# An early copy of the next scores, and a gate that turns its tokens where the FFN summed them

## The chip, the cores and the metric

The kernel runs on one core of a Trainium2 chip. Its metric is the device time of one execution, in microseconds. In three runs the kernel before took 1214.4, 1216.44 and 1218.95 us, so its median is 1216.44 us. One more execution, the profiled one, took 1221.99 us; its program spans 1220.3 us.

## The reference, cut to what matters

Three stages follow one another on 2304 tokens of width 512: attention in which each query keeps its 32 largest scores (4 batches, 8 heads, 576 positions, head width 64), a feed-forward layer (FFN, 512 to 2048 to 512, with a slope for negative values), and a mixture of 8 experts with one expert per token, chosen by a gate.

```python
scores = q @ k.T / sqrt(D)                       # 576 x 576 for each of 32 heads
kth    = 32nd largest of each row
attn   = softmax(where(scores >= kth, scores, -1e9))
x      = (attn @ v) as 2304 x 512
h      = x @ w_in;  x2 = (max(h, 0) + alpha * min(h, 0)) @ w_out
logits = x2 @ w_gate + bias[modality]            # 2304 x 8
e      = argmax(logits);  out = p(e) * (relu(x2 @ w1[e]) @ w2[e])
```

## The kernel before, in words

**Steps.** The attention is cut into 72 steps of two tiles each; a tile is 128 queries of one head against 576 keys. The work of a tile is spread over several steps, so that each step holds a piece of work of five different pairs of tiles. The order of the instructions is written out by hand: the schedule is manual, each engine executes its own instructions in the order of the program, and semaphores hold an instruction back until what it reads is written and what it overwrites has been read. Nothing is reordered.

The FFN runs in the same loop. It works on chunks of 256 tokens (two row blocks r = 0, 1), eight of them, and two half chunks of 128 tokens. A full chunk takes eight steps, one pair of hidden blocks (`fp`) a step, so that a chunk ends in about every eighth step. After the loop the expert phase runs, about 25 us for each of nine blocks.

**One step s** of the main loop holds, in the order of the program (the letters in front are engines: PE for TensorE, ACT for ScalarE, DVE for VectorE, POOL for GpSimd):

- POOL `low` (L530, L531) for the two tiles of step s-2 and a transposing DMA; ACT `mask` (L518) and POOL `mask` (L519) for the two tiles of step s-1
- DVE `topk` of the pair s, about 30 instructions: three L466 that read the score banks `SC` and the copied scores `t.S` (the first writes its result into `SC`, columns 576 to 719), two L463, then maxima and replacements (L469, L493)
- DVE `slope` (L657), ACT and POOL `pair` (L664, L665) for the FFN's hidden block of the step before
- PE `mm2` (L678) for the hidden block of two steps before; where the chunk is complete, ACT `fin` (L685) copies the two sums `c.X2[r]` to `c.x2`
- PE `scores` (L445, L446) for the pair s+1, into the two halves of `SC`; PE `mm1` (L629) for the next hidden block, into the bank `psH`
- ACT `expo` (L522) for the two tiles of s-1; ACT `relus` (L643), which copies `psH`; ACT `keep_scores` (L449), which copies the scores of the pair s+1 from `SC` to `t.S`; ACT `high` (L526) for the two tiles of s-1
- the slot "mid", with what earlier steps put there (the gate, parts of the preparation of q, k and v); PE `av` (L550) for the pair s-3; the slot "late"

So DVE's first instruction on a pair waits for `keep_scores` of that pair, POOL's `low` of the next step waits for `high`, and the second exponential waits for the second mask of POOL.

**The FFN's sums.** `c.X2[r]` is one tile of 128 x 512 fp32 from the pool `psX`, which has two buffers. The next chunk's first `mm2` takes the same buffers, as soon as their last reader is through.

**The gate** turns each row block of `c.x2` by four PE transposes (`gate1`, L690), copies the result to SBUF (L692, ACT) and multiplies it by the gate's weights (`logits`, L696). Before, `gate1` writes the turned tokens to columns 720 to 975 of `SC`, 256 columns in each half. Row block 0 is turned in the slot "mid" of the step after the chunk's end, row block 1 one step later; `logits` follow one step after each. The copies go to the ring `gr` of four buffers, which `relus` uses too. For the last two chunks `gate1` is called for both row blocks together, in `after` and in `finish`.

Of the kernel before, what the change touches and what calls it, by code (L numbers as in the profile page):

```python
# [14 lines left out]
AF = mybir.ActivationFunctionType  # L15
# [45 lines left out]
def tile_kernel(ctx, tc, q, k, v, w_in, w_out, alpha, mod_id, w_gate, mod_bias, w1, w2, out, dbg=None, force=False):  # L61
    nc = tc.nc
    V, A, G, T, SY = nc.vector, nc.scalar, nc.gpsimd, nc.tensor, nc.sync
# [5 lines left out]
    bankO = psO.tile([128, 512], F32, name="bankO")  # L69

    SC = psO.tile([128, 2, 1024], F32, name="psS")
    X2AT, GATEAT = 576, 720
    SUMS, LOGITS, RANKS, COUNTS = 264, 272, 288, 304
    psH = ctx.enter_context(tc.tile_pool(name="psH", bufs=1, space=PSUM))
    psX = ctx.enter_context(tc.tile_pool(name="psX", bufs=2, space=PSUM))
# [7 lines left out]
    ident = const.tile([128, 128], F32, name="ident")  # L83
# [91 lines left out]
    def phase1(exact, ph, rc, rs, flags, ohs, mp):  # L175
# [15 lines left out]
        def at(slot, s_, f):  # L191
            hooks[slot].setdefault(s_, []).append(f)

        def hooked(slot, s_):
            while hooks[slot].get(s_):
                hooks[slot][s_].pop(0)()
# [25 lines left out]
        def flush():  # L222
            while fill:
                fill.pop(0)()
# [223 lines left out]
        def keep_scores(t):  # L448
            A.activation(t.S, SC[:, t.z, :S], AF.Copy, scale=LOWER)  # L449
# [71 lines left out]
        def expo(t):  # L521
            A.activation(t.S, t.S, AF.Exp, scale=t.c.negc, bias=t.b)  # L522
# [65 lines left out]
        def chunk(ci, xn, rs):  # L588
            ffn = state.ffn
            c = Rec()  # L590
# [94 lines left out]
                    A.activation(c.x2[:, r, :], c.X2[r], AF.Copy, scale=c.un[:, r:r + 1])  # L685

            def gate1(r):
                p_ = SC[:, :, GATEAT:GATEAT + 256]
                for cc in range(NCC):
                    T.transpose(p_[:, cc // 2, cc % 2 * 128:cc % 2 * 128 + 128], c.x2[:, r, cc * 128:cc * 128 + 128], ident)  # L690
                c.x2T[r] = ffn.tile([128, NCC, 128], F32, name="gr", bufs=GR)
                A.activation(c.x2T[r].rearrange("p (a c) t -> p a (c t)", a=2), p_, AF.Copy)  # L692

            def logits(r):
                for cc in range(NCC):
                    T.matmul(bankO[:, LOGITS + 8 * r:LOGITS + 8 * r + 8], c.x2T[r][:, cc, :], wg[:, cc, :],  # L696
                             start=(cc == 0), stop=(cc == NCC - 1))
# [64 lines left out]
            def place(r):  # L762
                G.memset(spacer, 0.0)
                d_ = G.indirect_dma_start(out=mapD, out_offset=bass.IndirectOffsetOnAxis(ap=c.si[:, r:r + 1], axis=0),
                                          in_=c.tg[:, r, :], in_offset=None)
                if r:
                    tc.declare_no_dep(d_.ins, c.placed.ins, reason="other slots")
                c.placed = d_
# [14 lines left out]
            def after(s_):  # L783
                if c.k == NCH:
                    return
                if c.k == NCH - 1:
                    for r in range(2):
                        gate1(r)
                        at("next", s_ + 1, lambda r=r: logits(r))
                    at("next", s_ + 1, gate2)  # L790
                    at("next", s_ + 1, gate2b)
                    at("mid", s_ + 1, gate3)
                    at("mid", s_ + 1, gate3b)
                    at("mid", s_ + 1, weight)
                    at("mid", s_ + 1, inverse)
                    at("late", s_ + 1, flush)
                    for r in range(2):
                        at("late", s_ + 1, lambda r=r: place(r))
                    at("mid", s_ + 2, lambda: first_block(s_ + 2))
                    return  # L800
                for r in range(R):
                    at("mid", s_ + 1 + r, lambda r=r: gate1(r))
                    at("mid", s_ + 2 + r, lambda r=r: logits(r))
                at("mid", s_ + GATE[0], gate2)
                at("mid", s_ + GATE[0] + 1, gate2b)
                at("mid", s_ + GATE[1], gate3)
                at("mid", s_ + GATE[1] + 1, gate3b)
                at("mid", s_ + GATE[2], weight)
                at("mid", s_ + GATE[2] + 1, inverse)
                for r in range(R):  # L810
                    at("late", s_ + GATE[2] + 2 + r, lambda r=r: place(r))
# [77 lines left out]
        def weights_for(fp):  # L889

            return wgroup.cn["high"] >= 2 * fp + 18
# [135 lines left out]
        s_ = -LOOK  # L1027
        while True:
            att_on = s_ < NIT + 4
            if s_ == NIT + 4:  # L1030
                atts.close()
            if not att_on and not (posted or paired or fpq or any(x >= s_ for h_ in hooks.values() for x in h_ if h_[x])):
                break
            state.alone = s_ >= NIT
            k1_, main = 0, []

            def run_main(n_):
                nonlocal k1_
                for _ in range(n_):
                    if k1_ < len(main):  # L1040
                        main[k1_]()
                        k1_ += 1

            prev = live.get(s_ - 1, [])
            if WL == 0 and s_ < 12:
                wgroup.load()
            hooked("early", s_)
            while factors:
                factors.pop(0)()
            for t in live.get(s_ - 2, []):  # L1050
                low(t)
            for t in prev:
                mask(t)
            while doubt:
                doubt.pop(0)()
            main = topk(live[s_]) if 0 <= s_ < NIT else []
            if WL == 1 and s_ < 12:
                wgroup.load()
            hooked("next", s_)

            run_main(MAIN0)
            if ended:
                kept_, fill[:] = fill[:], []
                while ended:
                    av_out(ended.pop(0))
                flush()
                fill[:] = kept_
            post = posted[:]
            del posted[:]
            for c, fp in post:  # L1070
                for f in c.slope(fp):
                    f()
            for c, fp in paired:
                if c.k == NCH and fp == c.n - 1:
                    mp.b0.mm(0, (0,))
                c.mm2(fp)
                if fp == c.n - 1:
                    c.fin()
                    at("mid", s_, lambda c=c, s_=s_: c.after(s_))
                    at("late", s_, c.keep)  # L1080
            del paired[:]
            for c, fp in post:
                c.pair(fp)
                paired.append((c, fp))
            nxt = []
            if s_ + LOOK < NIT:
                nxt = live[s_ + LOOK] = tile_pair(s_ + LOOK)
                for t in nxt:
                    scores(t)
            while fill and FILL0:  # L1090
                fill.pop(0)()
                run_main(1)
            n_ = 0
            credit = min(credit + (RATE[2] if s_ < NIT else 1), 1 if s_ >= NIT else 1 if exact else CRED) if fpq else 0
            while fpq and credit >= 1 and n_ < 2 and fpq[0][0] <= s_ and weights_for(fpq[0][2]):
                credit -= 1
                _, c, fp = fpq.pop(0)
                c.mm1(fp)
                posted.append((c, fp))
                n_ += 2 if fp == c.n - 1 else 1  # L1100
            hooked("gap", s_)
            def rel(x):
                if x == (0 if state.alone else REL):
                    for c, fp in posted:
                        c.relus(fp)

            rel(0)
            while k1_ < len(main) or fill:
                run_main(1)
                if fill:  # L1110
                    fill.pop(0)()
            for t in prev:
                expo(t)
                if t is prev[0]:
                    rel(1)
            rel(2)
            for t in nxt:
                keep_scores(t)
            for t in prev:
                high(t)  # L1120
                if t is prev[0]:
                    rel(3)
            rel(4)
            if WL == 2 and s_ < 12:
                wgroup.load()
            hooked("mid", s_)
            for t in live.get(s_ - 3, []):
                av(t)
                u = t.u
                if t is u.last:  # L1130
                    ended.append(u)
                    if u.ready is not None:
                        at("late", s_ + 1, lambda u=u, s_=s_: start_chunk(*u.ready, s_ + 1))
            live.pop(s_ - 3, None)
            hooked("late", s_)
            wstep(WEARLY.get(s_, WSTEP))
            s_ += 1
# [218 lines left out]
```

## Time and profile before

| | us |
|---|---|
| median of three runs | 1216.44 |
| the profiled execution | 1221.99 |
| its span | 1220.3 |

| engine | busy us | share of the span |
|---|---|---|
| PE | 867.5 | 71% |
| PE weight loads | 639.2 | 52% |
| DVE | 874.9 | 72% |
| ACT | 787.5 | 65% |
| POOL | 706.3 | 58% |

The shares are means over stages that differ. From 0 to 59 us nothing but preparation runs. From 59 to 295 us attention steps run beside the conversion of the FFN's weights; from 295 to 836 us attention and FFN run together (with preparation of q, k and v again between 583 and 732 us); from 836 to about 990 us the FFN and the gate are finished; after that the expert phase runs. In the trace an instruction's idle time before it is put down to what ended the wait.

### The profile page before, as it was taken

What the parts mean: (1) busy time and instruction counts of PE and PEld (TensorE: products, weight loads), DVE (VectorE), ACT (ScalarE), POOL (GpSimd) and SP (SyncE); (2) the same over time, 40 slices, a digit from 0 to 9 for tenths busy, and PEclk for the clock granted to TensorE, in tenths of its full rate; (3) what the DMA queues carried; (4) which work ended last, traced back from release to release, by engine and by line L of the source; (5) the groups of instructions that cost most, each with busy time, mean ns of one, the idle gap of its engine ahead of it and who ended that gap; (6) DMA issues with size and microseconds to landing.
All of it is one profiled execution on the core that took longest, in us unless ns stands there. A gap on an engine that the chain in (4) does not pass through costs nothing.

```text
span 1220.3 us, 22434 instructions
## 1 busy us (share of the span) xinstructions
PE 867.5 (71%) x7484; PEld 639.2 (52%) x7484; DVE 874.9 (72%) x2842; ACT 787.5 (65%) x1288; POOL 706.3 (58%) x1090
## 2 busy tenths in 40 slices
PE   0212231336888888688778778879998989999996
PEld 0001111224556555455555446657665878888885
DVE  5888989778798989979778688993234365555540
ACT  5546795989887777768788677784324254544441
POOL 4266576688887878878788798796232212111110
PEclk9996555668999999889889789999999799999998
DMA  8969965777766656755879477553004298666600
GB/s 257 258 155 228 251 139 138 178 146 166 168 156 133 143 116 129 149 113 102 158 139 214 108 154 149 119 120 63 19 18 163 63 354 282 213 204 208 205 37 20
DMA packets 310488, 187.05 MB, mean 153 GB/s; under 512 B 246545, under 2 KB 279313, under 8 KB 310362
## 3 DMA queue, kind: packets, MB, share of 16 engines
q1 hardware_dynamic: 306586, 175.02, 59.8%
q0 software_dynamic: 3776, 10.51, 2.5%
q8 instruction: 60, 0.98, 0.3%
q14 instruction: 66, 0.54, 0.1%
HBM read 98.20 MB, written 25.94 MB: 102 GB/s over the span
## 4 chain that ended last, share of the span: by engine, by line
PE 35%; ACT 13%; POOL 13%; issue 6%; DMA 5%; DVE 4%; SPq 1%; POOLq 0%; ACTq 0%
PE psS L1293 9%; PE psX L1312 8%; POOL S L519 6%; PE psX L678 6%; PE psH L629 5%; ACT S L449 4%; PE psS L629 3%; ACT HL L526 3%; POOL HL L530 2%; DMA w<-in_moe_w_dram 1%; PE bankO L550 1%; ACT S L522 1%; PE psS L445 1%; ACT u L518 1%; POOL g L665 1%
## 5 line engine op out<-in xcount | busy, mean ns | idle before, releaser
L519 POOL TENSOR_TENSOR S<-u,S 128x576 f32<-128x576 bf16 x144 | 187.9, 1326 | 86.3 <-ACT u L518 86.3
L678 PE MATMUL psX<-Wo,g 128*128 128x512 f16 x864 | 212.2, 395 | 20.0 <-POOL g L665 19.7
L629 PEld LDWEIGHTS <-Wi 128*128 128x128 f16 x1920 | 175.2, 101 | 51.3 <-issue 16.3
L445 PE MATMUL psS<-QK 128*128 128x512 f16 (+1 forms) x160 | 65.5, 448 | 179.6 <-DVE B L463 148.7
L530 POOL TENSOR_TENSOR HL<-S,HL 128x512 f16<-128x512 f32 x144 | 168.0, 1166 | 31.9 <-POOL bc L498 14.2
L629 PE MATMUL psH<-xT,Wi 128*128 128x256 f16 (+1 forms) x1488 | 160.3, 267 | 15.7 <-DVE gr L657 15.7
L445 PEld LDWEIGHTS <-QK 128*128 128x128 f16 (+1 forms) x320 | 32.7, 111 | 244.5 <-DVE B L463 104.0
L522 ACT ACTIVATE S<-S,bc,nb 128x576 f32<-128x576 f32 x144 | 123.3, 864 | 58.0 <-POOL S L519 57.1
L678 PEld LDWEIGHTS <-g 128*128 128x128 f16 x864 | 82.2, 102 | 117.5 <-POOL g L665 27.7
L469 DVE MAX8 m<-X 128x8 f32<-128x160 f32 x432 | 117.3, 313 | 0.0
L665 POOL TENSOR_TENSOR g<-gr,g 128x512 f16<-128x512 f32 x72 | 84.1, 1168 | 57.1 <-ACT g L664 51.7
L1320 POOL DMA_INDIRECT out_dram<-o,ids x20 | 20.0, 998 | 161.3 <-ACT o L1318 159.6
L518 ACT ACTIVATE u<-S,bc 128x576 bf16<-128x576 f32 x144 | 103.2, 767 | 9.9 <-POOL bc L498 9.9
L1301 DVE SCALAR_TENSOR_TENSOR gl<-psS,gh 128x512 fp32r<-128x512 f32 x40 | 27.6, 691 | 99.5 <-ACT gh L1300 75.1
L526 ACT ACTIVATE HL<-S 128x576 f16<-128x576 f32 x144 | 91.3, 688 | 11.9 <-DMA PT<-HL 11.8
L1300 ACT ACTIVATE gh<-psS 128x512 fp32r<-128x512 f32 x40 | 23.9, 596 | 109.6 <-PE psS L1293 105.3
L449 ACT ACTIVATE S<-psS 128x576 f32<-128x576 f32 x144 | 85.0, 644 | 10.7 <-PE psS L446 10.7
L550 PEld LDWEIGHTS <-PT 128*128 128x128 f16 (+1 forms) x2240 | 86.5, 107 | 9.0 <-issue 7.5
L550 PE MATMUL bankO<-VV,PT 128*128 128x66 f16 (+1 forms) x2240 | 90.1, 203 | 0.7 <-DVE xh L577 0.6
L466 DVE SCALAR_TENSOR_TENSOR psS<-psS,S 128x288 f32<-128x288 f32 x72 | 33.2, 461 | 78.6 <-ACT S L449 50.1
L664 ACT ACTIVATE g<-gr 128x512 f16<-128x512 f32 x72 | 45.0, 624 | 64.9 <-DVE gr L657 36.3
L493 DVE MATCH_REPLACE8 X<-m,X 128x160 f32<-128x160 f32 x288 | 86.8, 309 | 0.0
(233 smaller groups left out, 2272.6 us busy)
## 6 DMA issues: line engine op xcount, KB each, us to landing
w<-in_moe_w_dram SPq DMA_DIRECT2D x80, 512.0 KB
qkD<-QK SPq DMA_DIRECT2D x16, 576.0 KB
QK<-qkD SPq DMA_DIRECT2D x16, 576.0 KB
wraw<-in_moe_w_in_dram SPq DMA_DIRECT2D x16, 512.0 KB
wraw<-in_moe_w_out_dram SPq DMA_DIRECT2D x16, 512.0 KB
vvD<-VV SPq DMA_DIRECT2D x16, 325.0 KB
VV<-vvD SPq DMA_DIRECT2D x16, 325.0 KB
K<-QK SPq DMA_DIRECT2D x32, 144.0 KB
```

The costliest lines, as they stand in the source:

```text
L445: T.matmul(ps[rows, 0:512], st, K[:, 4 * j:4 * j + 4, :], start=(n_ == 0), stop=(n_ == 1))
L449: A.activation(t.S, SC[:, t.z, :S], AF.Copy, scale=LOWER)
L469: ops.append(lambda: V.max(o, a_))
L518: A.activation(u, t.S, AF.Relu, scale=-BIG, bias=t.cut)
L519: G.tensor_tensor(t.S, u, t.S, op=ALU.subtract)
L522: A.activation(t.S, t.S, AF.Exp, scale=t.c.negc, bias=t.b)
L526: A.activation(t.HL.rearrange("p a b -> p (a b)")[:, 0:S], t.S, AF.Copy)
L530: G.tensor_tensor(f[:, 640:1152], t.S[:, 0:512], f[:, 0:512], op=ALU.subtract)
L550: T.matmul(oo, l, r, start=(n_ == 0), stop=(n_ == len(ops) - 1), skip_group_check=True)
L629: T.matmul(h[:, fb, :], Wi[:, 4 * cc + f0 // 512, wh, f0 % 512:f0 % 512 + 128], c.xT[:, :R, xh_, cc, :], start=(n == 0), stop=(n == 11))
L678: T.matmul(c.X2[r], g[:, gh, fb, r * 128:r * 128 + 128], Wo[:, FB * fp + fb, wh, :], start=(fp == 0 and fb == 0 and n == 0), stop=(fp == c ...
L1293: T.matmul(self.h[:, fb, :], w_[:, cc, 128 * fb:128 * fb + 128], x_[:, cc, :], start=(n == 0), stop=(n == 11))
```

## The change

Two edits. First, `keep_scores` for the pair s+1 moves from behind both exponentials and `relus` to the place between the first exponential and the second. Where no pair is in its exponentials yet, it stays in front of `rel(2)`.

Second, `gate1` turns its tokens into the tile `c.X2[r]` itself, whose sums `fin` has copied to `c.x2`, and no longer into `SC`. It runs for both row blocks in the slot "mid" of the step in which the chunk ends, and `logits` follow one and two steps later, a step earlier than before. The copy (L692) then reads 512 adjacent columns of one bank and no longer 256 columns of each of two.

```diff
-    X2AT, GATEAT = 576, 720
+    X2AT = 576
...
             def gate1(r):
-                p_ = SC[:, :, GATEAT:GATEAT + 256]
                 for cc in range(NCC):
-                    T.transpose(p_[:, cc // 2, cc % 2 * 128:cc % 2 * 128 + 128], c.x2[:, r, cc * 128:cc * 128 + 128], ident)
+                    T.transpose(c.X2[r][:, cc * 128:cc * 128 + 128], c.x2[:, r, cc * 128:cc * 128 + 128], ident)
                 c.x2T[r] = ffn.tile([128, NCC, 128], F32, name="gr", bufs=GR)
-                A.activation(c.x2T[r].rearrange("p (a c) t -> p a (c t)", a=2), p_, AF.Copy)
+                A.activation(c.x2T[r].rearrange("p c t -> p (c t)"), c.X2[r], AF.Copy)
...
                 for r in range(R):
-                    at("mid", s_ + 1 + r, lambda r=r: gate1(r))
-                    at("mid", s_ + 2 + r, lambda r=r: logits(r))
+                    gate1(r)
+                    at("mid", s_ + 1 + r, lambda r=r: logits(r))
...
             for t in prev:
                 expo(t)
                 if t is prev[0]:
                     rel(1)
+                    for t_ in nxt:
+                        keep_scores(t_)
+            if not prev:
+                for t in nxt:
+                    keep_scores(t)
             rel(2)
-            for t in nxt:
-                keep_scores(t)
             for t in prev:
                 high(t)
```

## Rows read from the trace of the kernel before

**Rows 1.** Busy time by stage: stage, length, PE, PEld, DVE, ACT, POOL, clock, DMA.

```profile
295.00:583.00 288.00, 235.16 (x2359) 156.70 (x2359) 256.96 (x1039) 222.55 (x362) 236.95 (x353) 0.96 0.65 139
583.00:732.00 149.00, 116.00 (x1189) 77.60 (x1188) 115.27 (x476) 118.65 (x199) 122.19 (x201) 0.89 0.76 152
```

**Rows 2.** Waits, whole span: who waited for whom, total us, times, longest.

```profile
ACT S L522 <- POOL S L519: 57.1, 96, 4.0
...
DVE psS L466 <- ACT S L449: 50.1, 34, 5.1
...
DVE psS L466 <- ACT gr L692: 28.3, 11, 4.8
...
ACT S L449 <- PE psS L446: 10.7, 3, 6.6
```

**Rows 3.** All of DVE's waits from 295 to 583 us.

```profile
DVE psS L466 <- ACT gr L692: 15.2, 6, 4.1
DVE psS L466 <- ACT S L449: 13.1, 14, 2.5
```

**Rows 4.** DVE's longest waits from 583 to 732 us.

```profile
DVE psS L466 <- ACT S L449: 10.5, 8, 2.9
DVE psS L466 <- ACT gr L692: 8.8, 3, 4.8
```

**Rows 5.** DVE's longest waits from 732 to 836 us.

```profile
DVE psS L466 <- ACT S L449: 4.5, 5, 2.0
DVE psS L466 <- ACT gr L692: 4.3, 2, 2.2
```

**Rows 6.** DVE's longest wait from 59 to 295 us.

```profile
DVE psS L466 <- ACT S L449: 17.0, 6, 4.4
```

**Rows 7.** Timeline, 350 to 378 us: start, duration, instruction [idle before it, releaser].

```profile
355.75 0.45 DVE L466 SCALAR_TENSOR_TENSOR psS<-psS,S 128x288 f32<-128x288 f32 x1
...
359.10 0.19 PE L446 MATMUL psS<-K,QK 128*128 128x64 f16 x1
...
360.46 0.87 ACT L522 ACTIVATE S<-S,bc,nb 128x576 f32<-128x576 f32 x1 [0.65 <-POOL S L519]
...
361.70 0.87 ACT L522 ACTIVATE S<-S,bc,nb 128x576 f32<-128x576 f32 x1 [0.38 <-POOL S L519]
...
362.48 0.58 ACT L643 ACTIVATE gr<-psH 128x512 f32<-128x512 f32 x1
...
362.96 1.18 ACT L449 ACTIVATE S<-psS 128x576 f32<-128x576 f32 x2
...
364.02 1.26 ACT L526 ACTIVATE HL<-S 128x576 f16<-128x576 f32 x2
364.17 0.47 DVE L466 SCALAR_TENSOR_TENSOR psS<-psS,S 128x288 f32<-128x288 f32 x1 [0.58 <-ACT S L449]
...
368.93 0.87 ACT L522 ACTIVATE S<-S,bc,nb 128x576 f32<-128x576 f32 x1
...
373.74 0.61 ACT L692 ACTIVATE gr<-psS 128x512 f32<-128x512 f32 x1
...
374.38 0.47 DVE L466 SCALAR_TENSOR_TENSOR psS<-psS,S 128x288 f32<-128x288 f32 x1 [1.49 <-ACT gr L692]
```

**Rows 8.** Timeline around 440 us, where a chunk ended at 431 us.

```profile
436.12 2.75 PE L678 MATMUL psX<-Wo,g 128*128 128x512 f16 x12
437.00 1.27 ACT L526 ACTIVATE HL<-S 128x576 f16<-128x576 f32 x2
...
441.92 0.87 ACT L522 ACTIVATE S<-S,bc,nb 128x576 f32<-128x576 f32 x1 [0.79 <-POOL S L519]
```

**Rows 9.** PE's timeline at the last chunk's gate.

```profile
946.46 0.66 PE L690 MATMUL psS<-ident,x 128*128 128x128 f32 x4 [1.41 <-DVE gl L1301]
...
949.60 1.22 PE L1293 MATMUL psS<-xth,w0h 128*128 128x256 f32 x4 [0.69 <-ACT gr L692]
```

**Rows 10.** ACT's groups of instructions: busy us, mean ns of one, idle before.

```profile
L384 ACT ACT_TABLE_LOAD x1 | 1.3, 1283 | 4.8 <-DMA rawq<-in_q_dram 4.8
```

## The prediction

> **What bounds the kernel now.** I read the busy time by stage first, then the table of waits, then DVE's waits stage by stage, then single steps in the timeline, and last the gates of the last two chunks.
>
> By stage no engine stands out. From 295 to 583 us DVE is busy 256.96 of 288 us, POOL 236.95, PE 235.16, ACT 222.55; from 583 to 732 us all four have between 115 and 123 of 149 us [rows 1]. So a chain through several engines bounds the loop, and the question is who waits last. For DVE the answer is short: from 295 to 583 us it waits 28.3 us in all, always before L466, its first instruction on a pair of tiles: 13.1 us for `keep_scores` (L449) and 15.2 us for the gate's copy (L692) [rows 3]. Busy time and these waits make 285.3 of the 288 us, so DVE is otherwise without a gap. Over the whole span the two waits come to 50.1 and 28.3 us, 78.4 together [rows 2].
>
> The timeline shows how a step closes. ACT starts the first exponential at 360.46, waits 0.38 us for POOL's second mask, starts the second at 361.70, then `relus` at 362.48, the two copies of scores at 362.96 and `high` at 364.02; the next first exponential starts at 368.93 [rows 7]. That is 8.47 us round the loop ACT, POOL (`low`, then the masks, which need `high`), ACT. DVE's L466 at 364.17 waited 0.58 us for the copies [rows 7]. Both loops are coupled by the copies, which stand late in ACT's order.
>
> **The early copy.** No instruction is added; all copies but the first four move. Back to back, an exponential takes 0.78 us from start to start (361.70 to 362.48), `relus` 0.48 and the two copies 1.06 [rows 7]. In the new order the first copy starts at 360.46 + 0.78 = 361.24 in place of 362.96: 1.72 us earlier for DVE. The second exponential starts at 361.24 + 1.06 = 362.30, 0.60 late, but POOL's mask is done at 361.70, so its wait of 0.38 is filled with work. `relus` starts at 363.08 and `high` at 363.56 in place of 364.02: 0.46 us earlier. The loop through ACT and POOL falls from 8.47 to 8.01 us.
>
> What is late next is DVE itself. From 355.75 to 364.17 it has 8.42 us with 0.58 of wait, from 364.17 to 374.38 it has 10.21 us with 1.49 of wait [rows 7]: 7.84 and 8.72 us of work (every second step also finishes an output), 8.28 on average. So a regular step costs about 8.28 us, set by DVE, and the early copy alone gives a fifth of a us in each, until a gate's step comes.
>
> The later things: nothing but `high` and POOL's correction, a step later, needs the second exponential. `relus` is 0.60 us late (363.08 for 362.48); its reader on DVE (`slope`) comes after the next L466, so it has over 2 us. The copy itself now needs the scores earlier. The last score matmul starts at 359.10 and takes 0.19 us [rows 7]; the copy will ask at 361.24, so the cover is 1.95 us. In the old place ACT waited for scores three times in the whole span, 10.7 us [rows 2]; these waits stay and the second exponential now stands behind them, at about 0.8 us each time. If the cover is gone in a step, that step loses what is missing, since everything of ACT stands behind it.
>
> **The gate.** It keeps its 72 transposes and 18 copies. It loses the waits that came from sharing the tile `SC`: L690 stood behind `keep_scores`, and L466 behind the copy (28.3 us over eleven gates [rows 2]), although none of the columns are shared. With the sums' own bank neither wait has a reason.
>
> What it adds is a wait of `mm2`: the next chunk's first `mm2` now needs the copies, which ACT makes after `high`. In the step around 440 us `high` starts at 437.00 and runs 1.27 us [rows 8], the gate's first copy would be done about 0.6 us later. With `high` 0.46 us earlier that is 438.4, and `mm2`, which started at 436.12, starts 2.3 us late and ends near 441.1. Behind it in PE's queue stand the scores, about 1 us, done at 442.1. The copy of these scores wants them 0.78 us after a first exponential that was at 441.92 and will be near 441.4: at 442.2. So it just fits; `mm1` and with it `relus` come some 0.5 us late for two or three steps, which the loop of 8.01 us against 8.28 recovers. Two copies in one step delay the masks' first half by 0.6 us in that step, beside POOL's `low`, which lasts longer. I take the new wait at nothing on the path; its upper bound is 2.3 us in each of three steps at nine chunk ends, 62 us (a rival below); below nothing it can't be, as a wait gains nothing.
>
> At the end of the FFN, PE alone sets the time, and the gate's waits are on it: 1.41 us before the last chunk's transposes and 0.69 us before the expert's matmuls at 949.60 [rows 9]; four more of 0.69 us stand at the gates of the last three chunks. I count 4.9 us; the lower end is 2 (if copies stay in PE's way), the upper 8, as the matmuls at 949.60 ran at the long duration of 1.22 us for four.
>
> **The sum**, against the profiled execution's 1221.99 us:
> - 295 to 583 us: 28.3 us of DVE's waits. The ends are 0 and 28.3. Single waits for `keep_scores` average 0.94 us (13.1 over 14), below the 1.72 that it comes earlier, and those for L692 go; but with 28 us less, PE would be busy 235.16 of 260 us and POOL 236.95 [rows 1], nine tenths, and some waits come back. I take 20.
> - 732 to 836 us: 4.5 + 4.3 = 8.8 us of the same kind [rows 5]: 6.
> - 583 to 732 us: 19.3 us [rows 4]. Here ACT (118.65) and POOL (122.19) are busier than DVE (115.27) [rows 1], and their preparation of q, k and v is unchanged: I take 7, between 0 and 19.
> - 59 to 295 us: 17.0 us [rows 6], in steps without `relus`, with DVE converting weights as they are loaded: 4, between 7 (six waits at 0.78 + 0.38 us) and a loss of 2 (the exponentials behind late scores).
> - the end: 5.
>
> That is 42 us: 1180 against 1221.99. The profiled execution is 0.46% above the median, so against 1216.44 the same share gives 1174.6; I say 1175 us.
>
> **A rule against it.** The first exponential is now followed by two `Copy` instructions and then by the second exponential. One load of activation tables stands in the trace, 1283 ns at the very start [rows 10], while each step already goes from Relu to Exp to Copy and on to Relu. So no load follows from the order, and I price the change of function at 0. The Trainium skill (ScalarE: Activation LUTs, "Table sets: the hidden batching unit") says that a load is due whenever the next function is in another set, and that cheap functions such as copy are in every set. By its first half alone the new order would cost two more loads in each of 70 steps; by both halves it costs nothing, as the trace has it.
>
> **Rivals.**
> - *All of DVE's waits go.* 78.4 us and 5 at the end: 1139, median 1134. For it: DVE's gap-free work. Against: POOL and PE at nine tenths, and the stages where ACT and POOL have more to do. Chance of over 62 us of gain: 0.08.
> - *A small gain or none.* The waits come back at other places (POOL's masks, `mm2`'s wait for L665), and the end's 5 us stay: 1217, median 1211 or more. For it: four engines within a few per cent from 583 us on. Against: the loop of 8.01 us. Chance of a gain of 6 to 20 us 0.06, of nothing 0.07.
> - *Slower.* The scores become what ACT waits for at each chunk's end. The late `mm2` delays them, the copy in front of the second exponential holds back `high`, that holds back POOL's `low` and masks, and the next step starts late. At 2.3 us in each of three steps at nine ends this costs 62 us, more than the 42 gained: 1242, median 1236. It decides from the point at which scores come more than 1.95 us later than now. For it: my margin at 442 us is 0.1 us. Against: DVE has 1.7 us in hand behind the copy. Chance 0.04.
> - *Table loads.* Two of 1283 ns in 70 steps, 180 us: 1402, median 1396. Against it stands the one load of the whole trace. Chance 0.01.
>
> The forecast itself, a gain of 20 to 62 us, has the remaining 0.74. Faster by over 0.5% (about what a measurement can tell from no change, 6 us): 0.74 + 0.08 + 0.06 = 0.88; within it 0.07; slower 0.05. The range from 1153 to 1204 us leaves out the slower cases, most of the small gains and the largest.
>
> **What would show it.** Right: L466's waits for L449 and L692 fall from 78.4 us to under 25; the second exponential waits for POOL no more; steps near 8.3 us around 360 us; the first `mm2` of a chunk starts some 2 us after `av`, with L692 as its releaser; no second table load. Wrong: L449 waits for L446 in many steps, or DVE's waits stand before other instructions in the same sum.

## The result and the profile after

The changed kernel takes 1176.76 us (median of four runs, 1172.66 to 1180.02) against 1215.62 us beside it: ratio 0.9669, 95% interval 0.9636 to 0.9701. The profiled executions span 1174.5 and 1220.3 us, 45.8 us apart. A second measurement gave 0.9672 (0.9653 to 0.9691).

The table takes both traces apart at the first exponential of the same steps (columns: forecast gain, then the length before, after, the gain, and the gain in the second profile of the changed kernel, in us).

| stretch before | forecast | before | after | gain | second profile |
|---|---|---|---|---|---|
| start to 295 us | 4 | 295.0 | 293.4 | 1.6 | 2.9 |
| 295 to 583 us | 20 | 288.1 | 268.7 | 19.4 | 20.5 |
| 583 to 732 us | 7 | 148.4 | 143.2 | 5.2 | 5.3 |
| 732 to 835 us | 6 | 103.8 | 94.7 | 9.1 | 5.7 |
| 835 us to the end | 5 | 385.0 | 374.5 | 10.5 | 11.2 |
| sum | 42 | 1220.3 | 1174.5 | 45.8 | 45.6 |

The two profiles of the changed kernel differ by up to 3.4 us in one stretch, so a single row is known to a few us only.

The busy time of the long stage, after (columns as in [rows 1]):

```profile
293.00:562.00 269.00, 233.21 (x2364) 155.76 (x2361) 256.02 (x1039) 219.79 (x363) 236.30 (x353) 0.96 0.70 148
```

The work is the same within 3 us on each engine and the granted clock is the same 0.96; only idle time went. DVE is now busy in 256 of 269 us, and three engines are above 85%.

The gain is not spread over the whole stage. Its first six steps, ahead of the first chunk's end, take 56.9 us before, 57.1 after, and 55.9 in the second profile. Nearly all of the gain stands in the 25 steps behind them. First before, then after:

```profile
351.88:583.14 231.26, 190.74 (x1973) 129.65 (x1972) 210.47 (x859) 175.00 (x286) 185.52 (x282) 0.96 0.61 128
350.49:562.11 211.62, 185.35 (x1960) 126.38 (x1959) 207.95 (x851) 172.22 (x285) 184.44 (x282) 0.98 0.67 139
```

In these steps L466 waits 18.5 us before and 0.3 us after. The second profile has 211.67 us for them, so two executions agree here within 0.1 us.

The table of waits of the changed kernel, whole span:

```profile
ACT S L522 <- POOL S L519: 54.3, 56, 4.1
...
DVE psS L466 <- ACT S L449: 34.6, 19, 5.4
...
ACT S L449 <- PE psS L446: 17.0, 7, 8.0
...
PE psX L678 <- ACT gr L692: 11.7, 6, 2.7
```

Against [rows 2]: L466's wait for L692 is gone (28.3 us), its wait for L449 fell from 50.1 to 34.6 us, 26.6 of it outside the long stage. L449 waits for scores 7 times instead of 3. The exponentials' wait for POOL kept its total and lost 40 of its 96 cases: the second exponential's wait was filled (from 24.5 us to 0.4) and the first one's grew (from 32.6 us to 54.0). The timeline of ACT shows where:

```profile
350.49 0.87 ACT L522 ACTIVATE S<-S,bc,nb 128x576 f32<-128x576 f32 x1 [1.27 <-POOL S L519]
...
358.47 0.87 ACT L522 ACTIVATE S<-S,bc,nb 128x576 f32<-128x576 f32 x1 [0.65 <-POOL S L519]
359.24 1.17 ACT L449 ACTIVATE S<-psS 128x576 f32<-128x576 f32 x2
360.30 0.86 ACT L522 ACTIVATE S<-S,bc,nb 128x576 f32<-128x576 f32 x1
361.06 0.59 ACT L643 ACTIVATE gr<-psH 128x512 f32<-128x512 f32 x1
361.54 1.26 ACT L526 ACTIVATE HL<-S 128x576 f16<-128x576 f32 x2
362.68 1.09 ACT L692 ACTIVATE gr<-psX 128x512 f32<-128x512 f32 x2
```

This is the same step as in [rows 7], and a chunk's end. The copies start 0.77 us after the first exponential, the second exponential follows without a wait, `high` starts at 3.07 us in place of 3.56, and one step to the next takes 7.98 us. The gate's two copies follow `high` in the same step. DVE's first L466 of the two pairs around them, without any wait:

```profile
353.13 0.45 DVE L466 SCALAR_TENSOR_TENSOR psS<-psS,S 128x288 f32<-128x288 f32 x1
...
360.89 0.44 DVE L466 SCALAR_TENSOR_TENSOR psS<-psS,S 128x288 f32<-128x288 f32 x1
```

The next chunk's end, on PE:

```profile
428.78 1.04 PE L690 MATMUL psX<-ident,x 128*128 128x128 f32 x8
429.66 1.03 PE L550 MATMUL bankO<-VV,PT 128*128 128x66 f16 x28
432.18 2.75 PE L678 MATMUL psX<-Wo,g 128*128 128x512 f16 x12 [1.49 <-ACT gr L692]
...
435.50 0.38 PE L445 MATMUL psS<-K,QK 128*128 128x512 f16 x1
```

and on ACT:

```profile
431.53 1.08 ACT L692 ACTIVATE gr<-psX 128x512 f32<-128x512 f32 x2
...
436.05 1.17 ACT L449 ACTIVATE S<-psS 128x576 f32<-128x576 f32 x2
...
438.56 0.60 ACT L643 ACTIVATE gr<-psH 128x512 f32<-128x512 f32 x1 [0.59 <-PE psH L629]
```

All eight transposes run in one go; the next `mm2` waits 1.49 us for the copies, the last score matmuls start at 435.50, and L449 takes the scores at 436.05 without a wait, 0.2 us after they are done. `relus` then waits 0.59 us for the late `mm1`. Behind none of the six waits of `mm2` in this trace does L449 wait for scores in the next step. In the second profile it does behind one, where `mm2` took 4.33 us and not 2.75 (at a granted 0.62), and L466 then waits 1.86 us for the copy:

```profile
716.66 4.33 PE L678 MATMUL psX<-Wo,g 128*128 128x512 f16 x12 [2.29 <-ACT gr L692]
...
722.12 1.19 ACT L449 ACTIVATE S<-psS 128x576 f32<-128x576 f32 x2 [1.81 <-PE psS L446]
```

The last chunk's gate on PE, after (the lines that answer to [rows 9]):

```profile
905.73 1.03 PE L690 MATMUL psX<-ident,x 128*128 128x128 f32 x8
907.30 0.74 PE L1296 MATMUL psS<-xth,w0h 128*128 128x256 f32 x4 [0.54 <-DVE gl L1304]
...
908.84 1.85 PE L696 MATMUL bankO<-wg,gr 128*128 128x8 f32 x16
```

Before, PE stopped three times at this gate (1.41, 0.69 and 0.69 us); now one stop of 0.54 us is left. The matmuls behind it are shorter too: four took 1.22 us, now 0.74. The granted clock around both gates goes with that. First the kernel before:

```profile
946.00:950.00 4.00, 2.17 (x10) 1.54 (x11) 0.40 (x1) 1.19 (x2) 0.00 (x0) 0.68 0.12 50
950.00:958.00 8.00, 8.00 (x39) 8.00 (x39) 1.39 (x8) 0.22 (x1) 0.00 (x0) 0.50 0.00 0
```

and the changed kernel:

```profile
907.00:913.00 6.00, 5.53 (x47) 5.38 (x48) 1.92 (x11) 1.32 (x4) 0.24 (x2) 1.00 0.06 23
```

Before, PE was busy 2.17 of 4 us at the gate, and in the 8 us behind it the granted clock was 0.50, the lower level (1.2 GHz); after, it stays at 1.00 here. From the expert's matmuls ahead of the gate (end 945.04, after 905.89) to the gate's first instruction on DVE (L710 at 955.78, after 910.73) it is 10.7 us before and 4.8 after. So this gate has 5.9 of the 10.5 us that the end gained: 2.2 are fewer stops and 3.7 are shorter work. Another 3.8 us lie ahead of it, from the last exponential on, and were not taken apart.

The lower level is not gone from the changed kernel. Behind the gate before the last, where all eight transposes run in one go too, twelve matmuls of `mm2` took 4.44 us (2.75 us at the same place before), at a granted 0.50 from 861 to 863 us.

### The profile page after: what moved, and what is told of

It reads as the page before. It is cut to its first block, busy times and chain, and to the rows that moved or that the text cites. A ratio compares the mean times of both kernels' runs of the same rounds, so it can differ in the third digit from the quotient of the medians.

```text
span 1174.5 us, 22450 instructions
## 1 busy us (share of the span) xinstructions
PE 852.5 (73%) x7484; PEld 628.1 (53%) x7484; DVE 870.5 (74%) x2842; ACT 780.0 (66%) x1288; POOL 701.2 (60%) x1090
## 4 chain that ended last, share of the span: by engine, by line
PE 32%; POOL 17%; ACT 16%; DVE 12%; DMA 10%; issue 7%; SPq 3%; POOLq 0%; ACTq 0%; DVEq 0%
PE psS L1296 9%; PE psX L1315 8%; PE psX L678 6%; POOL S L519 6%; POOL HL L530 3%; ACT HL L526 3%; PE psS L629 3%; ACT S L522 3%; PE psH L629 3%; DMA rawk<-in_k_dram 2%; DMA PT<-HL 2%; POOL g L665 2%; ACT S L449 2%; ACT u L518 2%; DVE m L469 2%
## 5 line engine op out<-in xcount | busy, mean ns | idle before, releaser
L678 PE MATMUL psX<-Wo,g 128*128 128x512 f16 x864 | 218.1, 403 | 39.9 <-POOL g L665 28.0
L629 PEld LDWEIGHTS <-Wi 128*128 128x128 f16 x1920 | 170.4, 99 | 41.2 <-DVE gr L657 13.2
L629 PE MATMUL psH<-xT,Wi 128*128 128x256 f16 (+1 forms) x1488 | 157.6, 265 | 7.0 <-DVE gr L657 7.0
L522 ACT ACTIVATE S<-S,bc,nb 128x576 f32<-128x576 f32 x144 | 124.3, 864 | 54.5 <-POOL S L519 54.3
L449 ACT ACTIVATE S<-psS 128x576 f32<-128x576 f32 x144 | 84.3, 635 | 17.2 <-PE psS L446 17.0
L466 DVE SCALAR_TENSOR_TENSOR X<-psS,S 128x288 f32<-128x288 f32 (+1 forms) x144 | 80.7, 602 | 2.5
L445 PE MATMUL psS<-K,QK 128*128 128x512 f16 (+1 forms) x160 | 64.8, 441 | 6.2 <-DMA K<-QK 6.2
```

The source lines that it names most:

```text
L445: T.matmul(ps[rows, 0:512], st, K[:, 4 * j:4 * j + 4, :], start=(n_ == 0), stop=(n_ == 1))
L629: T.matmul(h[:, fb, :], Wi[:, 4 * cc + f0 // 512, wh, f0 % 512:f0 % 512 + 128], c.xT[:, :R, xh_, cc, :], start=(n == 0), stop=(n == 11))
L678: T.matmul(c.X2[r], g[:, gh, fb, r * 128:r * 128 + 128], Wo[:, FB * fp + fb, wh, :], start=(fp == 0 and fb == 0 and n == 0), stop=(fp == c ...
```

## The experiments

Ratios are to the kernel before on the same chip, with 95% intervals; the changed kernel's is 0.967.

**The early copy alone.** The gate as before; only the last piece of the diff.

```diff
                 if t is prev[0]:
                     rel(1)
+                    for t_ in nxt:
+                        keep_scores(t_)
...
-            for t in nxt:
-                keep_scores(t)
```

> The early copy alone; the gate stays in SC at its old times. My theory (DVE's gaps before L466 are the loss, and each edit closes its own): the 50.1 us of waits for L449 fall below 30, those for L692 (28.3) fall only by what high comes earlier, 0.46 us a time, to some 22; the end of the FFN gains nothing. 1198 us, between 1190 and 1205. Rival (the gate's waits were the whole loss, the copy was hidden): 1212 or more. Rival (both edits are needed, as the early copy of the scores is what the gate's transposes waited for): the copy alone gives over 30 us, below 1186.

Measured: 1198.36 us, ratio 0.9815 (0.9781 to 0.9848). DVE's waits:

```profile
DVE psS L466 <- ACT S L449: 25.4, 14, 5.0
DVE psS L466 <- ACT gr L692: 22.6, 11, 6.2
```

As my theory had it, in time and in both waits. The end gains nothing: from the last exponential to the end it takes 389.1 us (385.0 before), and the last gate has its stops still (1.42, 0.69 and 0.69 us), with a granted 0.50 in the 9 us behind it.

**The gate alone.** The changed kernel with the copies back in their old place.

```diff
-                    for t_ in nxt:
-                        keep_scores(t_)
...
+            for t in nxt:
+                keep_scores(t)
```

> The gate in the sums' banks alone; the copies stay behind both exponentials. My theory: L692 no longer stands before L466 (28.3 us gone), the waits for L449 stay near 50, the end of the FFN gains its 10 us, and a chunk's first mm2 waits some 2.8 us for the copies, hidden for the most part: 1188 us, between 1180 and 1196. Rival (late mm2 makes the scores late and eats the gain): 1205 or more. The sum of the gains of both edits alone should be within 8 us of the 39 us of both together if they close separate waits.

Measured: 1202.85 us, ratio 0.9863 (0.9831 to 0.9895), short of the range that I had given. Its waits:

```profile
DVE psS L466 <- ACT S L449: 66.2, 42, 5.6
...
ACT S L522 <- POOL S L519: 60.8, 104, 4.0
...
PE psX L678 <- ACT gr L692: 10.3, 5, 2.7
```

L466 no longer waits for L692, but its waits for L449 grew by 16 us, in the long stage by 8 us and six cases, as many as gates stood there: the gate's copy had been the last of two things that were late. The end has the gain, 373.0 us, and that is 12.0 of the 22.2 us between the spans of this profile and the one before. The gains of the two edits alone, 1.85% and 1.37%, make 3.22%, and both together give 3.31%: they add up. So they do in the 25 steps from 352 us on: the early copy alone takes 219.8 us there (11.5 less than before), the gate alone 223.8 (7.4 less), both 211.6 (19.6 less).

**The new times with the old bank.** The changed kernel, but the tokens are turned in `SC` again.

```diff
-                    T.transpose(c.X2[r][:, cc * 128:cc * 128 + 128], ...
+                    T.transpose(p_[:, cc // 2, cc % 2 * 128:cc % 2 * 128 + 128], ...
```

> The changed kernel with its new times of the gate, but the tokens turned in SC as before. If sharing SC was the cost (my theory), L466 waits for L692 again, twice at each chunk's end in one step, the second transposes wait for the first copy, and the FFN's end loses its gain: 1205 us, between 1195 and 1215. Rival (the earlier time and not the bank is what helped): within 5 us of the changed kernel's 1177.

Measured: 1208.76 us, ratio 0.9911 (0.9877 to 0.9946). Its waits:

```profile
DVE psS L466 <- ACT S L449: 28.8, 18, 5.0
DVE psS L466 <- ACT gr L692: 24.5, 7, 4.8
...
PE psS L690 <- ACT gr L692: 15.8, 8, 3.3
```

This kernel and the changed one differ in the bank alone, so the bank is the point and not the earlier time: with the bank shared, the gate's copies hold L466 again, the second transposes wait for the first copy, and the end takes 387.4 us. It is even slower than the early copy with the gate at its old times (1198.36 us). The sums' bank at the old times was not tried.

**Copies in front of both exponentials.** The changed kernel with the two copies one place earlier still.

```diff
+            for t in nxt:
+                keep_scores(t)
             for t in prev:
                 expo(t)
                 if t is prev[0]:
                     rel(1)
-                    for t_ in nxt:
-                        keep_scores(t_)
...
```

> The changed kernel with the copies in front of the first exponential. The copies then fill the first exponential's wait for POOL (0.65 to 2 us in regular steps of the changed kernel) and high could come 0.5 us earlier, but the scores must be there 0.78 us sooner (cover 1.95 us less 0.78, less what E0 waits). If DVE sets the steps now (my theory): within 6 us of 1177. If the loop ACT-POOL still sets them: 1155 or less. If late scores are what ACT meets: 1185 or more, with L449 waiting for L446 in most steps.

Measured: 1170.86 us, ratio 0.9596 (0.9550 to 0.9641).

```profile
ACT S L449 <- PE psS L446: 42.4, 18, 12.1
...
DVE psS L466 <- ACT S L449: 19.0, 12, 5.4
ACT S L522 <- POOL S L519: 14.3, 28, 1.1
```

It fills the first exponential's wait too (54.3 to 14.3 us) and pays with waits for scores (17.0 to 42.4 us). The long stage falls from 268.7 to 262.1 us in these profiles; in the second pair, of the last experiment below, from 267.6 to 264.4. In the 25 steps from 352 us on both pairs agree: 2.4 us less. The time lies at the edge of what I had for no change (within 6 us of 1177) and far from the 1155 of the rival; with the repetition below it is 8.3 us. So DVE did not set all steps: most of the waits of L466 that went (34.6 to 19.0 us) stood outside those 25 steps, which had 0.3 us of them.

**More work for DVE.** The maximum F is taken twice.

```diff
                 tt(F[:, :, 0:h2], X1, X2, ALU.max)
+                tt(F[:, :, 0:h2], X1, X2, ALU.max)
```

> The changed kernel with one instruction of DVE more in each step: the maximum F (L463) is taken twice, some 0.36 us from start to start, 26 us over 72 steps; the result is the same. If DVE's work sets the steps now (my theory), most of it shows: the changed kernel's ratio of 0.967 rises by 15 to 26 us, to some 0.981 to 0.988. If the loop through ACT and POOL sets them, DVE's spare time takes it: under 8 us.

> The same doubled maximum in the kernel before. There DVE has 78 us of waits before L466, 0.58 us in a regular step, so my theory has it hidden in part: the copies' time, not DVE's, starts L466 in about half of the steps. 6 to 16 us slower, ratio 1.005 to 1.013. If DVE's work set the steps before too: 20 us or more.

Measured: in the changed kernel 1209.93 us, ratio 0.9942 (0.9918 to 0.9966), 33 us more; in the kernel before 1236.86 us, ratio 1.0162 (1.0130 to 1.0193), 20 us more. The first is above what I had for either theory, the second above mine and at the lower edge of the rival's 20 us or more. The trace of the first shows a wait that neither kernel has without the doubled maximum (the other one has it too, 49.6 us):

```profile
DVE B L463 <- PE psS L446: 59.6, 44, 4.1
```

The program takes five instructions of `topk` ahead of the scores. With one more, B slipped behind the scores in program order; it reads `SC`, which they write, and waited. So neither run measures DVE's work alone, and I repeated the one on the changed kernel with six.

```diff
-MAIN0 = 5
+MAIN0 = 6
...
+                tt(F[:, :, 0:h2], X1, X2, ALU.max)
```

> The doubled maximum again, with one instruction more ahead of the scores (MAIN0 = 6): with 5 the next instruction, B, had slipped behind the scores' matmuls and waited for them (59.6 us in that kernel's trace), so its 33 us were not DVE's work alone. Now 0.36 to 0.45 us of DVE work a step is all that is added, 26 to 32 us over 72 steps. If DVE's work and the loop ACT-POOL both bound the changed kernel within some per cent (my theory by now): 12 to 24 us slower than the changed kernel, ratio 0.977 to 0.987. If DVE's work alone bounds: over 24. If the loop alone: under 6.

Measured: 1186.43 us, ratio 0.9753 (0.9731 to 0.9775). On the same chip the changed kernel took 1176.61, so the added work (DVE is busy 32 us longer) cost 9.8 us, less than the 12 that I had as the lower end. DVE's waits took up part of it:

```profile
DVE psS L466 <- ACT S L449: 21.4, 15, 5.0
```

**Less work for DVE.** 24 largest scores in place of 32, so one round of maxima and replacements less.

```diff
-KTOP = 32
+KTOP = 24
```

> The changed kernel keeps the 24 largest scores and not 32: one of four rounds of maxima and replacements is left out, 1.04 us of DVE in each step (four rounds start 1.04 us apart in the trace). If DVE sets the steps now, they fall to the next bound, the loop of 7.97 us through ACT and POOL: 8 to 25 us faster than the changed kernel, 1152 to 1169. If DVE does not: within 5 us of 1177.

Measured: the program's second, exact pass, which it takes when the quick selection leaves a doubt, ran behind the first. I had not foreseen that, and the span of 2562.1 us has both. The first pass alone can be read: its long stage takes 266.7 us, where the changed kernel takes 268.7. First its busy time, columns as in [rows 1]:

```profile
290.00:556.00 266.00, 234.55 (x2379) 157.37 (x2376) 226.74 (x860) 218.85 (x361) 235.28 (x353) 0.95 0.71 149
```

and L466's wait in that stage:

```profile
DVE psS L466 <- ACT S L449: 34.7, 28, 3.2
```

DVE lost 29 us of work (256.02 to 226.74) and got 27 us of waiting (8.0 us in the changed kernel). So in the changed kernel DVE's work alone does not set the long stage. The steps show it one by one: three regular ones from 342 us on take 7.97, 7.98 and 7.97 us in the changed kernel, and 7.99, 7.99 and 7.98 us with 24 largest.

**Both reliefs.** Copies in front of both exponentials, and 24 largest; one execution.

> Copies in front of the first exponential and the 24 largest scores, both together; a second, exact pass runs behind the first, so only the first pass is read, from the step of 295 us to that of 562 us of the changed kernel (31 steps: 268.7 us there; 262.1 with the copies in front; 266.7 with 24 largest). If two bounds stand close together, relieving both gives more than the sum of 6.6 and 2.0: 255 us or less. If a third (PE, POOL's total of 237) stands right behind: 258 to 261.

Measured: 259.1 us for the long stage of the first pass.

```profile
289.00:547.00 258.00, 228.93 (x2356) 155.36 (x2357) 226.97 (x864) 218.51 (x360) 233.74 (x351) 0.97 0.73 152
```

The gain is 9.6 us, against 6.6 and 2.0 alone. Two profiles of one kernel differ by 1.1 and 2.3 us in this stage, so I read the sum from the 25 steps from 352 us on (in the numbers of the kernel before), where they agree. In this order: the doubled maximum in its place, 24 largest, copies in front (the second profile), and both reliefs:

```profile
347.71:569.58 221.87, 186.94 (x1961) 126.11 (x1959) 218.88 (x876) 172.21 (x285) 184.31 (x282) 0.98 0.65 135
346.59:556.52 209.93, 187.42 (x1968) 128.26 (x1967) 185.47 (x710) 171.95 (x286) 184.26 (x282) 0.97 0.68 139
349.75:558.98 209.23, 184.00 (x1965) 126.05 (x1964) 206.45 (x844) 172.80 (x286) 185.01 (x282) 0.98 0.70 141
340.30:547.62 207.32, 187.19 (x1970) 128.19 (x1969) 184.67 (x706) 172.93 (x286) 184.36 (x282) 0.97 0.71 141
```

Against 211.62 us, 24 largest gives 1.7 us, the copies in front 2.4, and both 4.3: about the sum, and no more. For the whole stage I had set 255 or less for two bounds side by side; it came out in the range for a third one right behind. POOL (233.74 of 258, 91%), PE (89%) and DVE (88%) are then about equally full; which of them it is was not tried.

The first row tells the other half. 10.9 us more work of DVE made these steps 10.3 us longer, nearly all of it; 22.5 us less made them 1.7 us shorter. So DVE's work does set their time in the changed kernel, and a second bound stands within 1% behind it.

**One copy on each side.**

```diff
+            late_ = nxt[:]
+            if late_:
+                keep_scores(late_.pop(0))
             for t in prev:
                 expo(t)
                 if t is prev[0]:
                     rel(1)
+                    while late_:
+                        keep_scores(late_.pop(0))
...
```

> The changed kernel with one copy of scores before the first exponential and one behind it. With both in front (1170.9) L449 waited 42 us for scores; with one in front the first exponential's wait for POOL takes one copy only and the scores have 0.5 us more. If DVE's work is the bound, it can't be much under 1171: 1166 to 1176. If ACT's waits for scores cost time there: 1163 or less.

Measured: 1169.62 us, ratio 0.9614 (0.9581 to 0.9647), no different from both in front. L449 still waits 41.0 us for scores, so the run does not tell what those waits cost.

**The two best, side by side**, five executions each: the changed kernel as it is, and the copies in front.

> The changed kernel as it is, beside the next run on the same chip: ratio 0.967 as before, between 0.963 and 0.971.

> The kernel with both copies in front of the first exponential again, with five rounds, to tell whether it beats the changed kernel: 4 to 9 us faster than it, ratio 0.957 to 0.964. If the first measurement was luck: within 3 us of the changed kernel.

Measured: 1176.61 us, ratio 0.9672 (0.9653 to 0.9691), and 1168.27 us, ratio 0.9584 (0.9565 to 0.9602). The intervals are apart: with the copies in front of both exponentials the kernel is 8.3 us faster than the changed one.

## Why the prediction was right, and where it was not

- **The total** (1175 forecast, 1176.76 measured; 42 and 45.8 us in the traces). The mechanism is the one forecast: the edits take waits from an in-order chain and leave the work alone. The two edits alone show it, each with its own gain, and the gains add up. The waits themselves do not: the gate's copy ended 15.2 us of L466's waits in the 25 steps from 352 us on, and without it these steps were 7.4 us shorter, as L466 then waited for L449 (11.4 us for 3.3).
- **The early copy.** Step by step as forecast: copies 1.73 us earlier (1.72 forecast), second exponential without a wait, `high` 0.49 us earlier (0.46 forecast), a loop of 7.98 us (8.01).
- **What is late next.** Here I was wrong in part. I had DVE alone set a regular step at 8.28 us, with the loop through ACT and POOL 0.27 us below. In the 25 steps from 352 us on DVE is indeed busy 8.32 of 8.46 us a step, and more work of it shows nearly in full (10.3 of 10.9 us). But the steps around 360 us take 7.97 us, not 8.3, and less work gave 1.7 of 22.5 us: the loop (8.01 forecast) bounds as much as DVE does.
- **The long stage's size** (19.4 for 20) is in part luck. I had let 8 of the 28.3 us of waits come back because PE and POOL would be at nine tenths. 8.0 us are left, but 7.7 of them stand in the six steps ahead of the first chunk's end, where L466 had waited 9.8 us and the early copies gave little (57.1, 55.9 and, with the early copy alone, 54.5 us for 56.9); behind them 0.3 are left, with PE and POOL at 88 and 87%. What holds the copies back in those six steps is open.
- **The waits that stay.** L466 still waits 34.6 us where I had said under 25; 16.5 of it stand before 295 us, where it had been 22.1 (17.0 of them in [rows 6], 5.1 ahead of 59 us). I take it that what precedes the exponential is late there; no run shows it. That stage gave 1.6 and 2.9 us for 4 forecast, and 0.1 with the early copy alone. That is no more than executions differ by: the gate alone, which changes nothing up to there, has 298.2 us for 295.0.
- **The cover of the scores** held: seven waits in 70 steps, 17.0 us for 10.7. The longest, 8.0 us for 6.6, stands in a step in which the kernel before waited too, and the second exponential stood behind it, as forecast.
- **The gate's new wait.** Forecast 2.3 us at each end; measured 11.7 us over six, 1.95 each, with scores 0.2 us ahead of the copy where I had 0.1. That nothing of it reaches the path holds in the first profile, where no wait for scores follows, but not in the second, where 1.86 us of one wait came to L466. No run took the wait away alone, so its price is not shown. The late `mm1` cost `relus` 0.59 us in that step (0.5 forecast).
- **The end** is the term that I sized wrongly: 4.9 us forecast, 10.5 and 11.2 measured, above even my upper end of 8. I counted the stops and not what followed them: the eight us at the lower clock behind the last gate, where 3.7 us came from shorter work. I had seen the long matmuls at 949.60 and put them into the upper end only.
- The errors have both signs (in the first profile too much by 2.4 and 1.8 us in the stages with preparation, too little by 3.1 and 5.6 in the last two; in the second the stage from 732 us gave 5.7 for 6), so the total is closer than its terms, and that is luck.
- **Table loads:** one in the changed trace as before. That rival is out, as the trace had it.

## What to carry to other kernels

On an engine that works in program order, look for a wait between two instructions of a pair and put work there whose inputs are ready. Here that added no work, and what waited for the moved copies came 1.73 us earlier; its price was 6.3 us more of waits for scores in the whole span, so check first by how much the inputs are ahead. A scratch tile inside a buffer that others write and read makes all of them wait for each other, in both directions; a bank whose own work is just done is a better place, and its price is one wait of the next writer. Where several loops are equally long, relieving one gives a part only (1.7 us for 22.5 us less work), and the total of waits in front of one instruction is a ceiling, not a forecast: of 78.4 us, 35.3 came.

## What the runs showed that I had not expected

What followed the stops of the last gate on PE cost more than the stops: PE was busy 2.17 of 4 us, and the 8 us behind had a granted 0.50. It was so in the kernel before and in the traces of the early copy alone and of the new times in the old bank; with the sums' bank the clock stayed at 1.00 there in the traces of the changed kernel, the gate alone and the copies in front. That the stops made it fall is not shown: the changed kernel has the lower level behind the gate before the last, with its transposes in one go.

And one instruction that changes its place against another engine's can cost more than it runs: B, behind the scores and no longer ahead of them, waited 59.6 us in a kernel to which 28 us of work had been added.
